# Two weight loads in the place of a matrix not yet written, and a conversion one frame earlier, in a kernel of attention, soft experts and a feed-forward layer

## The chip, the cores and the metric

The kernel runs on one core of a Trainium2 chip. The metric is the time of one execution on the device, in microseconds. TensorE (PE) does the matrix products, VectorE (DVE), ScalarE (ACT) and GpSimd (POOL) the elementwise work, and SyncE (SP) issues nearly all transfers between the chip's memory (HBM) and the core's on-chip memory (SBUF). PE's results land in a small separate memory (PSUM).

## The reference

Attention over 4 batches and 8 heads (576 tokens, 64 channels) that keeps the 32 largest scores of each row, then a layer of 8 soft experts with 4 slots each, then a feed-forward layer on every token. `w_in` and `w_out` of the last one arrive as 64-bit floats.

```python
scores = scale * np.matmul(q, k.transpose(0, 1, 3, 2))
kth = np.partition(scores, -top_k, axis=-1)[..., -top_k:-top_k + 1]
attn = softmax(np.where(scores >= kth, scores, -1e9))      # then x = attn @ v
...
logits = x @ phi                                    # 2304 x 32
d = softmax(logits, axis=0); c = softmax(logits, axis=1)
h = np.maximum((d.T @ x)[e] @ w1[e], 0.0)           # each of 8 experts, 4 slots
slot_out[e] = h @ w2[e]
x = c @ slot_out
...
h = x @ w_in                                        # 512 x 2048
g = np.where(h >= 1, h, np.where(h <= -1, 0, (h + 1) ** 2 / 4))
return g @ w_out                                    # 2048 x 512
```

## The kernel before

**Attention.** The 32 heads are handled as 16 pairs. A table, `ORDER`, is one frame of a software pipeline written out by hand: each entry is an operation (a letter and numbers) and a last letter a, b or c, which says how many frames behind the newest pair that operation works. Frames 0 to 18 run it over the 16 pairs. On PE, ACT, DVE and POOL the order of the table is the order of the program there; the order of the rest, and that of the whole tail, is set by the tile framework's scheduler.

**The conversion of `w_in`.** Its 16 blocks of 128 x 512 are converted from 64-bit to 32-bit floats beside attention, one block a frame, by the entries c0 to c6: c0 and c1 on ACT (L213, L215), c2 on ACT (L217, which also issues the load of the next block into the buffer `x64`, L192), c3 on POOL (L219), c4 on DVE (L221), c5 and c6 on POOL (L223, L225). c6 also writes the converted block to HBM (`cv_d`, L205), whence it is loaded again later. `x64` and the result buffer `tr` are one each (the `cv_slots`).

**The weight loads.** `wload` loads the weights in a fixed list, `worder`, each load 512 KB, numbered w_0, w_1, ... 32 of `w1` (w_0 to w_31), 32 of `w2` (to w_63), then two of converted `w_in` (w_64, w_65), two blocks of `w_out` (w_66, w_67), six more of `w_in` (w_68 to w_73) and 14 more of `w_out`. All are issued by SP in this order, into places taken from the list `wfree`. During attention 13 places of their own exist (`slots_a`), and each frame issues two loads until they are full, in the seventh frame. The last pair frees further places: six buffers of the attention inputs at its operation S00, three more and a score buffer at X40, and a score buffer each at some T. After the loop come `cv_slots` (2) and `half_slots` (4); then attention closes (`att.close`, which waits for its last readers, PE's `moe_ps` of L618 among them) and three more places come free (`wB`). From there on `ring`, the list of places in the order they were filled, is used again from its start (L742).

**The tail.** PE computes the experts' first layer (`h1`, L804), their second (`so_0` and `so_1`, L823). Beside `so_1` runs `mix`: it transposes the logits (`lt_ps`, L764), makes their softmax on DVE and ACT, transposes the result (`c_ps`, L790), and ACT copies it into `cT`, the token-mix matrix, one tile of 128 x 2304 (9,216 bytes in each partition) that is allocated at the program's start. `m_first` (L841) multiplies the slots with a quarter of `w_in`, `m_rest` (L850) with the other three, and `m_spread` (L865) brings these into shape. The feed-forward layer is then 96 steps of a block of 384 tokens and a block f of 128 hidden units: `emit_g` makes `h_ps` on PE (L898, two PSUM buffers shared with the other small products), `rg` on ACT (L900, L901) and DVE (L902), and its high and low halves `ghl` on DVE (L904, L905); `emit_o` does nine products `o_ps` (L916). The first 32 steps alternate between two blocks of tokens. For each f, `wo_prep` converts a block of `w_out` (the same seven operations as above, on `tr_l` and `sg_l`) and splits it into `whl` (ACT L891, DVE L892), four blocks ahead (`CLA`).

## Time and profile before

| what | us |
|---|---|
| time before, median of three runs | 875.06 |
| lowest and highest of them | 874.54, 876.78 |
| span of the profiled execution | 872.0 |
| busy in it: PE, DVE, ACT, POOL | 821.5, 685.8, 644.8, 485.4 |

The span is the time from the first to the last instruction of one profiled execution; the median of the runs stands 3.06 us over it. In the timeline the frames of attention fill the span up to about 565 us, the experts' layers and the mix lie between 565 and 616, the first 32 steps of the feed-forward layer, in which `w_out` is converted, between 616 and 715, and the other 64 behind. A reader starts with the engines' shares, then asks in which stretch which engine waits, and for whom.

### The profile page before, as it was taken

To read this page: it belongs to the slowest core of one execution; us is meant where nothing else is said; L and a number is where in the kernel's file an instruction comes from. 1 tells how busy PE (TensorE), PEld (TensorE's weight loads), DVE (VectorE), ACT (ScalarE), POOL (GpSimd) and SP (SyncE) were. 2 spreads that over 40 slices of the span, in tenths; PEclk is the share of its full clock that TensorE was granted. 3 is DMA by queue.
4 is the path that set the end of the run, shared out by engine and by line. 5 is a ranking of instruction groups with operands and counts; after the bars stand their busy time and mean duration, and the time that the engine had idled before them with its cause. 6 is when DMAs were issued, how large, how long until landed. Compare 5 with 4: busy or idle time off the path is not lost.

```text
span 872.0 us, 17711 instructions
## 1 busy us (share of the span) xinstructions
PE 821.5 (94%) x5695; PEld 674.7 (77%) x5695; DVE 685.8 (79%) x3084; ACT 644.8 (74%) x1292; POOL 485.4 (56%) x494
## 2 busy tenths in 40 slices
PE   4889999999999999999999999799698899999996
PEld 3678989988989988988988988632266678888885
DVE  6999999988999989999989994103389995666663
ACT  5688999988998988998988987412578766545453
POOL 2577888877888877888877774100467740000000
PEclk9799999999999999999999999899799999999999
DMA  8453563553353353353452536699940001001001
GB/s 240 124 152 96 165 176 98 156 157 89 103 142 92 112 133 89 102 142 87 117 134 78 157 101 205 206 343 386 399 175 1 0 2 73 37 0 38 1 37 40
DMA packets 49461, 108.59 MB, mean 125 GB/s; under 512 B 8304, under 2 KB 8304, under 8 KB 49360
## 3 DMA queue, kind: packets, MB, share of 16 engines
q1 hardware_dynamic: 49040, 106.73, 40.2%
q8 instruction: 47, 0.77, 0.4%
q10 hardware_dynamic: 320, 0.66, 0.3%
q14 instruction: 54, 0.44, 0.2%
HBM read 70.70 MB, written 8.91 MB: 91 GB/s over the span
## 4 chain that ended last, share of the span: by engine, by line
PE 78%; DVE 10%; DMA 6%; ACT 3%; POOL 1%; issue 1%; ACTq 0%; POOLq 0%; SPq 0%; DVEq 0%
PE s_ps L311 20%; PE o_ps L916 17%; PE av_ps L485 14%; PE pt_ps L457 7%; PE s_ps L413 4%; PE av_ps L486 3%; PE rem_ps L230 3%; DMA w<-in_moe_w_dram 2%; DMA w<-in_moe_w_out_dram 2%; PE h L804 2%; DVE cand L338 2%; PE moe_ps L569 2%; DMA w<-cv_d 1%; PE h_ps L898 1%; PE xT_ps L534 1%
## 5 line engine op out<-in xcount | busy, mean ns | idle before, releaser
L311 PE MATMUL s_ps<-kh,q 128*128 128x288 f32 x640 | 208.1, 342 | 16.4 <-DVE q L266 9.0
L916 PE MATMUL o_ps<-whl,ghl 128*128 128x512 f32 x864 | 216.9, 395 | 5.0 <-DVE ghl L904 4.0
L916 PEld LDWEIGHTS o_ps<-whl,ghl 128*128 128x128 f32 x864 | 159.1, 188 | 44.7 <-DVE ghl L904 7.1
L445 POOL TENSOR_TENSOR ssb<-ssb,pen 128x576 f32<-128x576 f32 x141 | 180.4, 1284 | 18.3 <-ACT pen L442 15.8
L311 PE MATMUL s_ps<-kl,q 128*128 128x288 f32 x640 | 181.2, 299 | 0.0
L338 DVE MAX8 cand<-ssb 128x8 f32<-128x82 f32 (+1 forms) x1008 | 164.2, 228 | 5.0 <-ACT ssb L329 4.0
L311 PEld LDWEIGHTS s_ps<-kh,q 128*128 128x128 f32 x640 | 123.6, 193 | 34.7 <-DVE q L266 9.4
L485 PE MATMUL av_ps<-v_sb,ptb 128*128 128x65 f32 (+1 forms) x1280 | 147.1, 261 | 0.4 <-ACT xT L547 0.4
L485 PEld LDWEIGHTS av_ps<-v_sb,ptb 128*128 128x128 f32 (+1 forms) x1280 | 141.1, 181 | 5.2 <-issue 2.6
L311 PEld LDWEIGHTS s_ps<-kl,q 128*128 128x128 f32 x640 | 124.4, 194 | 0.3
L422 DVE MAX8 l<-s_ps 128x8 f32<-128x576 f32 x144 | 109.2, 758 | 18.3 <-PE s_ps L413 17.9
L442 ACT ACTIVATE pen<-ssb,kb 128x576 bf16<-128x576 f32 x141 | 110.3, 792 | 4.5 <-POOL kb L438 3.3
L329 ACT COPY ssb<-s_ps 128x576 f32<-128x576 f32 x144 | 91.1, 641 | 25.3 <-PE s_ps L311 21.8
L448 ACT ACTIVATE ssb<-ssb,nm 128x576 f32<-128x576 f32 x141 | 109.0, 785 | 0.6 <-POOL ssb L445 0.6
L900 ACT ACTIVATE rg<-h_ps,half 128x384 f32<-128x384 f32 x96 | 55.2, 579 | 71.0 <-PE h_ps L898 70.8
L396 POOL TENSOR_SCALAR mb<-ssb,top 128x576 bf16<-128x576 f32 x48 | 83.3, 1736 | 19.2 <-DVE top L345 9.2
L902 DVE SCALAR_TENSOR_TENSOR rg<-h_ps,rg 128x384 f32<-128x384 f32 x96 | 52.9, 554 | 47.4 <-ACT rg L901 47.1
L467 ACT COPY ptb<-pt_ps 128x512 f32<-128x512 f32 x144 | 82.4, 598 | 3.3 <-PE av_ps L485 3.3
L457 PE MATMUL pt_ps<-ident,ssb 128*128 128x128 f32 x576 | 84.3, 273 | 0.2
L398 DVE TENSOR_SCALAR_CACHE_REDUCE mb<-ssb,top 128x576 bf16<-128x576 f32 x96 | 75.8, 802 | 0.0
L345 DVE MAX8 top<-cand 128x8 f32<-128x56 f32 x432 | 73.5, 207 | 0.1
L457 PEld LDWEIGHTS pt_ps<-ident,ssb 128*128 128x128 f32 x576 | 68.7, 142 | 1.3 <-ACT ptb L467 0.8
(160 smaller groups left out, 1311.7 us busy)
## 6 DMA issues: line engine op xcount, KB each, us to landing
w<-in_moe_w_dram SPq DMA_DIRECT2D x60, 512.0 KB, 6.7
q<-qst SPq DMA_DIRECT2D x60, 160.0 KB, 3.1
kh<-kst SPq DMA_DIRECT2D x60, 144.0 KB, 2.5
kl<-kst SPq DMA_DIRECT2D x60, 144.0 KB, 2.9
x<-in_moe_w_in_dram SPq DMA_DIRECT2D x16, 512.0 KB, 3.9
w<-in_moe_w_out_dram SPq DMA_DIRECT2D x16, 512.0 KB, 9.3
v_sb<-in_v_dram SPq DMA_DIRECT2D x16, 325.0 KB, 2.9
raw_t<-in_q_dram SPq DMA_DIRECT2D x15, 320.0 KB, 3.7
```

The source lines that it names most:

```text
L311: nc.tensor.matmul(s[:, hf, :HS], a, w, start=(n == 0), stop=(n == len(terms) - 1), skip_group_check=True)
L329: nc.scalar.copy(st[u]["ssb"][:, j], st.pop((u, j))[:, :, :HS])
L338: nc.vector.max(st[u]["cand"][:, j, 8 * g:8 * g + 8], row(u, j)[:, S * g // NSEG:S * (g + 1) // NSEG])
L396: nc.gpsimd.tensor_scalar(st[u]["mb"][:, j], row(u, j), t_u, None, op0=ALU.is_ge)
L422: nc.vector.max(st[u]["l8"][:, j], st.pop((u, j))[:, :, :HS])
L442: nc.scalar.activation(pen, row(u, j), AF.Relu, bias=st[u]["kb"][:, j:j + 1], scale=-BIG)
L445: nc.gpsimd.tensor_tensor(row(u, j), row(u, j), st.pop((u, "pen", j)), op=ALU.subtract)
L448: nc.scalar.activation(row(u, j), row(u, j), AF.Exp, bias=st[u]["nm"][:, j:j + 1], scale=0.125)
L457: nc.tensor.transpose(pt[:, c, :], pr[:, c * P:(c + 1) * P], ident)
L467: nc.scalar.copy(ptb, st.pop((u, "pt", j)))
L485: nc.tensor.matmul(o, pj[:, c, sl], v_sb[:, 4 * jj + c, :], start=(c == 0), stop=False)
L916: nc.tensor.matmul(pos[t][n], a[:, sl], w, start=(f == 0 and k == 0), stop=(f == NF - 1 and k == 2))
```

## The change

Three things are changed.

The first conversion block begins one frame earlier: the entries c0, c1 and c3 go from b to a, and c2, c4, c5 and c6 from c to b. All 16 blocks move with it, so the last is finished one frame earlier, too.

When the last c6 has been written, the two `cv_slots` are given to `wfree` and loads are issued into them at once, in place of after the loop.

`cT` is split into two halves of 4,608 bytes in each partition, `cT0` and `cT1`, in a pool of their own, and they are allocated in `mix`, where they are first written. Up to there their places are two entries at the head of `wfree` (`loan`), so w_0 and w_1 are loaded into them. These two places are not put into `ring`.

```diff
--- before.py
+++ after.py
@@ -56,14 +56,14 @@
 NV = 2
 CLA = 4
 ORDER = '''
-Y30b z4b E00b Q30c A11c X21b P11b T40c S00a md M31b H1c A20c Y21b Q31c K20b c4c U01b E01b C00a
-G00a K21b K30b c2c L4b S01a Q40c U11b N3b C01a R4c X31b Y31b A21c E10b S10a T00b T01b G01a B2b
-c5c P21b M40b H2c P20b E11b C10a K31b L0a O40b U21b S11a C11a Q00b A30c N0a B3b M00a X40b G10a
-Q01b U20b R0b P30b G11a Y40b L1a M10a A31c T10b S20a H3c T11b c6c E20b E21b R1b N4b S21a M01a
+Y30b z4b E00b Q30c A11c X21b P11b T40c S00a md M31b H1c A20c Y21b Q31c K20b c4b U01b E01b C00a
+G00a K21b K30b c2b L4b S01a Q40c U11b N3b C01a R4c X31b Y31b A21c E10b S10a T00b T01b G01a B2b
+c5b P21b M40b H2c P20b E11b C10a K31b L0a O40b U21b S11a C11a Q00b A30c N0a B3b M00a X40b G10a
+Q01b U20b R0b P30b G11a Y40b L1a M10a A31c T10b S20a H3c T11b c6b E20b E21b R1b N4b S21a M01a
 C20a M11a A40c C21a Q10b A41c U30b N1a K40b H4c B4b X00a S30a Q11b P31b lDc Y00a T20b md G20a
 T21b z0a md lNc R2b C30a X10a lYc K00a P40b Y10a lEc lXc E30b X01a S31a O01a A00b A01b G21a
 U31b z1a lCc Y01a X11a E31b mc C31a Q20b L2a K01a Q21b G30a M20a z2a K10a md U40b Y11a md
-z3a H0b G31a S40a c0b T30b M21a c1b K11a L3a E40b T31b mc B0a P00a O21a mc c3b R3b C40a
+z3a H0b G31a S40a c0a T30b M21a c1a K11a L3a E40b T31b mc B0a P00a O21a mc c3a R3b C40a
 B1a X20a M30a P10a mc U00a U10a mc P01a N2a Y20a G40a A10b X30a
 '''.split()
 GA = 2
@@ -80,7 +80,7 @@
     make_identity(nc, ident)
     nbig = cpool.tile([P, P], BF16, name="nbig")
     nc.scalar.mul(nbig, ident, -BIG)
-    cT = cpool.tile([P, NT], F32R, name="cT")
+    p_ct = ctx.enter_context(tc.tile_pool(name="p_ct", bufs=1))
     lall = cpool.tile([P, S], F32, name="lall")
     acc = cpool.tile([P, P], F32, name="acc")
     run_s = cpool.tile([P, 1], F32, name="run_s")
@@ -128,7 +128,8 @@
     half_slots = [((p_hold, "xu", 1), (p_qkv, "v_sb", NV))] + [((p_hold, "mb", NMB),) * 2]
     half_slots += [((p_hold, "ptb", 4),) * 2] * 2
     ssb_slot = whole(p_ssb, "ssb", NSSB)
-    wfree = list(slots_a)
+    loan = [whole(p_ct, f"cT{n}", 1) for n in range(2)]
+    wfree = loan + slots_a
     ring = []
 
     def slot_tiles(slot, name, dtype):
@@ -145,7 +146,8 @@
             if slot is None:
                 return
             wfree.remove(slot)
-            ring.append(slot)
+            if slot not in loan:
+                ring.append(slot)
             full, parts = slot_tiles(slot, f"w_{wnext[0]}", I32 if l == 4 else F32)
             if l == 0:
                 src = w1[e, c * P:(c + 1) * P, :].rearrange("p (n f) -> p n f", n=2)
@@ -659,6 +661,9 @@
                 i = pi + min(pi, NWE) + (k == "d")
                 if i < NCV:
                     conv_op(i, int(name[1]))
+                    if (i, name[1]) == (NCV - 1, "6"):
+                        wfree.extend(cv_slots)
+                        wload(99)
         else:
             if name == "G00" and pi > 0:
                 return
@@ -711,7 +716,7 @@
             for name, k in order:
                 if 0 <= frame - k < NPAIR:
                     emit(name, frame - k)
-    wfree.extend(cv_slots + half_slots)
+    wfree.extend(half_slots)
     wload(99)
     run(moe_acc(B - 1, [(0, 2 * P), (2 * P, NR * P), (NR * P, S)], ps_s))
     siT = cpool.tile([P, NHP, NSLOT], F32, name="siT")
@@ -754,7 +759,10 @@
         axes = "abcd"[:len(shape) - 1]
         return t.rearrange(f"p ({' '.join(axes)}) -> p {' '.join(axes)}", **dict(zip(axes, shape[1:])))
 
+    cT = []
+
     def mix():
+        cT.extend(p_ct.tile([P, NT // 2], F32R, name=f"cT{n}", tag=f"cT{n}", bufs=1) for n in range(2))
         wide = [P, NR + 1, B, NSLOT]
         lt = mix_tile("lt", F32, wide)
         for rows in (range(NR), (NR,)):
@@ -789,7 +797,7 @@
                     n = P if r < NR else REM
                     nc.tensor.transpose(ps[:, r % NR, :n], c4[:n, r].rearrange("p a b s -> p (a b s)"), ident[:n, :n])
                 w = len(rows) * n
-                nc.scalar.copy(cT[:, b * S + rows[0] * P:b * S + rows[0] * P + w],
+                nc.scalar.copy(cT[b // 2][:, b % 2 * S + rows[0] * P:b % 2 * S + rows[0] * P + w],
                                ps.rearrange("p a b -> p (a b)")[:, :w])
 
     nc.vector.tensor_scalar_add(run_s, run_s, 1e-9)
@@ -895,7 +903,7 @@
     def emit_g(s_):
         t, f = s_
         ph = ps_m.tile([P, 512], F32, name="h_ps", tag="m_ps")[:, :BLK]
-        nc.tensor.matmul(ph, m4[f // 4][:, f % 4 * P:(f % 4 + 1) * P], cT[:, t * BLK:(t + 1) * BLK], start=True, stop=True)
+        nc.tensor.matmul(ph, m4[f // 4][:, f % 4 * P:(f % 4 + 1) * P], cT[t // 3][:, t % 3 * BLK:(t % 3 + 1) * BLK], start=True, stop=True)
         r, g = (x[:, :BLK] for x in ring_tile("g", g_slots, "rg", F32))
         nc.scalar.activation(r, ph, AF.Relu, bias=half, scale=0.5)
         nc.scalar.activation(r, r, AF.Square)
```

The line numbers of the changed kernel are greater by 2 from about L130 on, by 5 in the 700s, and by 8 from `mix` on.

The change moves instructions, as the programs' orders show. The first place is SP's queue at the end of attention, before and then after: `cv_d15` is the write of the last converted block, w_n a weight load.

```order
L167 DMA w_27_9209<-in_moe_w1_dram 128x1024
L167 DMA w_28_9288<-in_moe_w1_dram 128x1024
L205 DMA cv_d15_112<-tr_9166 128x512
L167 DMA w_29_9290<-in_moe_w1_dram 128x1024
L167 DMA w_30_9292<-in_moe_w1_dram 128x512
L167 DMA w_30_9293<-in_moe_w1_dram 128x512
L167 DMA w_31_9296<-in_moe_w1_dram 128x512
L167 DMA w_31_9297<-in_moe_w1_dram 128x512
L167 DMA w_32_9300<-in_moe_w2_dram 128x512
L167 DMA w_32_9301<-in_moe_w2_dram 128x512
L167 DMA w_33_9304<-in_moe_w2_dram 128x512
```

```order
L207 DMA cv_d15_114<-tr_8847 128x512
L169 DMA w_27_9092<-in_moe_w1_dram 128x1024
L169 DMA w_26_9088<-in_moe_w1_dram 128x1024
L169 DMA w_32_9298<-in_moe_w2_dram 128x512
L169 DMA w_32_9299<-in_moe_w2_dram 128x512
L169 DMA w_28_9094<-in_moe_w1_dram 128x1024
L169 DMA w_29_9140<-in_moe_w1_dram 128x1024
L169 DMA w_33_9302<-in_moe_w2_dram 128x512
L169 DMA w_33_9303<-in_moe_w2_dram 128x512
L169 DMA w_30_9199<-in_moe_w1_dram 128x1024
L169 DMA w_31_9224<-in_moe_w1_dram 128x1024
L169 DMA w_34_9306<-in_moe_w2_dram 128x512
```

The write of `cv_d15` now stands ahead of w_26 and w_27 where it stood behind w_28. w_32 and w_33 are issued in the midst of the w1 loads, into the conversion's two buffers.

The second place is PE in `so_1`, at the two parts of `lt_ps` (`so_sb` is the result of `so_0`), before and then after.

```order
L823 MATMUL so_1_9745<-w_49_9439,h1T_1_9619 32x512
L823 MATMUL so_1_9745<-w_50_9441,h1T_1_9619 32x512
L831 MATMUL soT_ps_9667<-ident_62,so_sb_9665 128x128 x4
L764 MATMUL lt_ps_9677<-ident_62,lall_70 128x128 x4
L823 MATMUL so_1_9745<-w_51_9443,h1T_1_9619 32x512
L823 MATMUL so_1_9745<-w_48_9437,h1T_1_9619 32x512
L823 MATMUL so_1_9745<-w_49_9439,h1T_1_9619 32x512
L823 MATMUL so_1_9745<-w_50_9441,h1T_1_9619 32x512
L823 MATMUL so_1_9745<-w_51_9443,h1T_1_9619 32x512
L232 MATMUL lt_ps_9683<-ident_62,lall_70 64x128
L230 MATMUL lt_ps_9683<-ident_62,lall_70 64x128
L823 MATMUL so_1_9745<-w_52_9445,h1T_1_9619 32x512
```

```order
L831 MATMUL so_1_9749<-w_51_9445,h1T_1_9621 32x512
L831 MATMUL so_1_9749<-w_48_9439,h1T_1_9621 32x512
L831 MATMUL so_1_9749<-w_49_9441,h1T_1_9621 32x512
L831 MATMUL so_1_9749<-w_50_9443,h1T_1_9621 32x512
L831 MATMUL so_1_9749<-w_51_9445,h1T_1_9621 32x512
L831 MATMUL so_1_9749<-w_52_9447,h1T_1_9621 32x512
L839 MATMUL soT_ps_9669<-ident_62,so_sb_9667 128x128 x4
L772 MATMUL lt_ps_9681<-ident_62,lall_72 128x128 x4
L831 MATMUL so_1_9749<-w_53_9449,h1T_1_9621 32x512
```

The transposes of `so_sb` and `lall` now stand behind a second round of products with w_48 to w_51 and the first with w_52. The transposes into `c_ps`, which stood among the products with w_56 to w_60, now stand behind the first with w_60 and later.

The third place is the start of the steps. On ACT, `rg` is the activation of a step, `tr_l` and `sg_l` belong to the conversion of w_out, before and then after:

```order
L843 CAST m4_0_9396<-m_ps0_9789 128x512
L891 CAST whl_9805<-tr_l_9796 128x512
L217 ACTIVATE sg_l_9809<-w_67_9477 128x512
L900 ACTIVATE rg_9846<-h_ps_9844,half_75 128x384
L900 ACTIVATE rg_9855<-h_ps_9853,half_75 128x384
L901 ACTIVATE rg_9846<-rg_9846 128x384
L901 ACTIVATE rg_9855<-rg_9855 128x384
L891 CAST whl_9817<-tr_l_9808 128x512
L900 ACTIVATE rg_9876<-h_ps_9874,half_75 128x384
```

```order
L851 CAST m4_0_9402<-m_ps0_9793 128x512
L908 ACTIVATE rg_9850<-h_ps_9848,half_77 128x384
L908 ACTIVATE rg_9859<-h_ps_9857,half_77 128x384
L909 ACTIVATE rg_9850<-rg_9850 128x384
L909 ACTIVATE rg_9859<-rg_9859 128x384
L899 CAST whl_9809<-tr_l_9800 128x512
L219 ACTIVATE sg_l_9813<-w_67_9479 128x512
L908 ACTIVATE rg_9880<-h_ps_9878,half_77 128x384
L909 ACTIVATE rg_9880<-rg_9880 128x384
L899 CAST whl_9821<-tr_l_9812 128x512
```

The four instructions on `rg` now stand ahead of the first `whl` cast. On PE, between the step (1,1) of the feed-forward layer, whose last products are the first row here, and the next steps, after:

```order
L924 MATMUL o_ps1_2_9930<-whl_9821,ghl_9925 128x512
L906 MATMUL h_ps_9974<-cT0_9678,m4_0_9402 128x384
L906 MATMUL h_ps_10004<-cT0_9678,m4_0_9402 128x384
L906 MATMUL h_ps_10022<-cT0_9678,m4_0_9402 128x384
L906 MATMUL h_ps_10053<-cT0_9678,m4_1_9403 128x384
L924 MATMUL o_ps1_0_9928<-whl_9833,ghl_9980 128x512 x2
```

Before, there was one `h_ps` at a time between the steps there:

```order
L916 MATMUL o_ps1_2_9926<-whl_9817,ghl_9921 128x512 x2
L898 MATMUL h_ps_9970<-cT_69,m4_0_9396 128x384
L916 MATMUL o_ps1_0_9924<-whl_9817,ghl_9921 128x512
L916 MATMUL o_ps1_1_9925<-whl_9817,ghl_9921 128x512
L916 MATMUL o_ps1_2_9926<-whl_9817,ghl_9921 128x512
L898 MATMUL h_ps_10001<-cT_69,m4_0_9396 128x384
L916 MATMUL o_ps0_0_9883<-whl_9829,ghl_9954 128x512 x2
L916 MATMUL o_ps0_1_9884<-whl_9829,ghl_9954 128x512 x2
```

Four `h_ps` now follow each other. The products of `m_rest` (`m_ps1`), which were 24 in a row, now have products `o_ps` of the first two steps between the last of them.

## Rows read from the trace of the kernel before

**Rows 1.** Two lines of the page: the busy share of the 16 DMA engines in 40 equal slices of the span (21.8 us each, in tenths), and the chain of work that ended last, by engine.
```profile
DMA  8453563553353353353452536699940001001001
...
PE 78%; DVE 10%; DMA 6%; ACT 3%; POOL 1%; issue 1%; ACTq 0%; POOLq 0%; SPq 0%; DVEq 0%
```

**Rows 2.** The table by stretches. A row has the stretch in us, its length, then busy us and number of instructions of PE, PE's weight loads, DVE, ACT and POOL, the clock granted to PE as a share of the full one, the busy share of the DMA engines, and GB/s.
```profile
28.00:60.00 32.00, 26.09 (x167) 20.62 (x166) 31.83 (x174) 26.75 (x49) 22.87 (x27) 0.93 0.35 95
...
544.00:552.00 8.00, 7.33 (x59) 6.43 (x59) 0.67 (x3) 4.86 (x13) 3.70 (x3) 1.00 0.44 131
...
575.00:590.00 15.00, 15.00 (x113) 4.68 (x106) 2.07 (x3) 2.75 (x4) 0.00 (x0) 1.00 1.05 389
...
615.00:620.00 5.00, 3.89 (x12) 1.86 (x12) 1.04 (x5) 3.45 (x6) 2.88 (x2) 1.00 1.04 388
620.00:625.00 5.00, 1.09 (x4) 0.30 (x2) 2.34 (x3) 1.40 (x3) 3.72 (x4) 0.81 1.05 394
625.00:630.00 5.00, 2.64 (x10) 0.86 (x13) 2.89 (x6) 4.55 (x10) 1.83 (x2) 0.50 1.03 411
630.00:635.00 5.00, 5.00 (x22) 1.44 (x16) 0.44 (x2) 1.03 (x3) 2.08 (x2) 0.66 1.03 409
...
651.00:711.00 60.00, 53.52 (x219) 39.46 (x220) 55.58 (x88) 46.75 (x88) 45.31 (x32) 1.00 0.00 1
```

**Rows 3.** What SP's DMA queue waited for between 556 and 570 us: us in total, times, longest.
```profile
SPq L167 <- PE moe_ps L618: 6.6, 1, 6.6
```

**Rows 4.** The timeline of SP's DMA queue from 556 to 640 us: start, us from the first issue of the row to the end of the last, line, what is loaded, how many.
```profile
556.49 45.10 SPq L167 DMA_DIRECT2D w<-in_moe_w_dram  x39
...
607.99 1.69 SPq L167 DMA_DIRECT2D w<-in_moe_w_out_dram  x2
```

**Rows 5.** The timeline of PE from 594 to 636 us: start, us, line, output and inputs, shape, how many; in brackets the idle time before the row and what ended it.
```profile
601.09 2.37 PE L823 MATMUL so<-w,h1T 128*32 128x512 f32 x12 [0.29 <-DMA w<-in_moe_w_dram]
603.90 1.05 PE L823 MATMUL so<-w,h1T 128*32 128x512 f32 x2 [0.44 <-DMA w<-in_moe_w_dram]
605.88 0.83 PE L790 MATMUL c_ps<-ident,c 128*128 128x128 f32 x5 [0.93 <-DVE c L784]
...
616.77 3.70 PE L841 MATMUL m_ps<-w,so 128*128 128x512 f32 x8 [0.71 <-DVE so L835]
622.41 0.62 PE L898 MATMUL h_ps<-cT,m 128*128 128x384 f32 x2 [1.94 <-DVE m L844]
627.36 0.69 PE L898 MATMUL h_ps<-cT,m 128*128 128x384 f32 x1 [4.33 <-DVE rg L902]
627.98 6.29 PE L850 MATMUL m_ps<-w,so 128*32 128x512 f32 x24
```

**Rows 6.** The timeline of ACT from 594 to 640 us, columns as before.
```profile
616.08 0.66 ACT L213 ACTIVATE tr_l<-w 128x512 f32<-128x512 f32 x1 [0.73 <-DMA w<-in_moe_w_out_dram]
...
624.19 0.62 ACT L891 CAST whl<-tr_l 128x512 fp32r<-128x512 f32 x1 [3.10 <-POOL tr_l L225]
...
625.28 1.03 ACT L900 ACTIVATE rg<-h_ps,half 128x384 f32<-128x384 f32 x2
626.20 0.92 ACT L901 ACTIVATE rg<-rg 128x384 f32<-128x384 f32 x2
```

**Rows 7.** Groups of PE's instructions between 651 and 711 us: line, operation, shape, how many | busy us, mean ns of one | idle us before them and what ended it.
```profile
L916 PE MATMUL o_ps<-whl,ghl 128*128 128x512 f32 x193 | 50.3, 401 | 4.2 <-DVE ghl L904 3.5 <-DVE ghl L905 0.2
L898 PE MATMUL h_ps<-cT,m 128*128 128x384 f32 x22 | 7.3, 346 | 2.4 <-DVE rg L902 2.4
```

**Rows 8.** The timeline of POOL from 700 to 713 us: the last product of the conversion of a w_out block.
```profile
710.52 1.17 POOL L225 TENSOR_TENSOR tr_l<-tr_l,sg_l 128x512 f32<-128x512 f32 x1
```

**Rows 9.** The timeline of ACT from 541 to 553 us: the first operation of the last conversion of w_in.
```profile
544.65 0.69 ACT L213 ACTIVATE tr<-x 128x512 f32<-128x512 f32 x1
```

**Rows 10.** The timeline of DVE from 548.2 to 549.5 us: DVE's operation of the same conversion.
```profile
548.49 0.43 DVE L221 TENSOR_SCALAR tr<-tr 128x512 int32<-128x512 int32 x1
```

**Rows 11.** The timeline of DVE from 30 to 42 us: the row with the longest idle time before it.
```profile
36.98 0.25 DVE L338 MAX8 cand<-ssb 128x8 f32<-128x82 f32 x1 [0.17 <-ACT ssb L329]
```

**Rows 12.** The timeline of POOL from 24 to 42 us: its first row.
```profile
26.54 1.73 POOL L396 TENSOR_SCALAR mb<-ssb,top 128x576 bf16<-128x576 f32 x1 [5.32 <-DVE top L345]
```

**Rows 13.** Groups of DVE's instructions between 720 and 860 us, where no w_out block is converted any more; columns as in the groups of PE.
```profile
L905 DVE TENSOR_TENSOR ghl<-rg,ghl 128x384 fp32r<-128x384 f32 x62 | 34.6, 558 | 2.1
L902 DVE SCALAR_TENSOR_TENSOR rg<-h_ps,rg 128x384 f32<-128x384 f32 x62 | 34.5, 557 | 42.6 <-ACT rg L901 42.6
L904 DVE CAST ghl<-rg 128x384 fp32r<-128x384 f32 x62 | 22.3, 360 | 4.4
```

**Rows 14.** The same for 634 to 711 us, beside the conversions on POOL.
```profile
L905 DVE TENSOR_TENSOR ghl<-rg,ghl 128x384 fp32r<-128x384 f32 x26 | 22.5, 868 | 0.6
L904 DVE CAST ghl<-rg 128x384 fp32r<-128x384 f32 x28 | 17.6, 634 | 1.1
```

**Rows 15.** The timeline of PE from 636 to 716 us: where the seventh step begins.
```profile
651.01 2.39 PE L916 MATMUL o_ps<-whl,ghl 128*128 128x512 f32 x9 [0.18 <-DVE ghl L905]
```

**Rows 16.** Groups of POOL's instructions between 610 and 712 us: the conversions of the 16 blocks of w_out.
```profile
L219 POOL TENSOR_SCALAR tr_l<-tr_l 128x512 f32<-128x512 f32 x16 | 26.0, 1627 | 76.3 <-ACT tr_l L213 76.3
L223 POOL TENSOR_TENSOR tr_l<-tr_l 128x512 int32<-128x512 int32 x16 | 22.0, 1374 | 10.9 <-DVE tr_l L221 8.6 <-ACT whl L891 1.3 <-ACT rg L901 1.1
L225 POOL TENSOR_TENSOR tr_l<-tr_l,sg_l 128x512 f32<-128x512 f32 x16 | 20.0, 1252 | 4.7 <-ACT sg_l L217 4.1
```

## The prediction

> **What bounds the kernel now.** I read the page first. In the chain of work that ended last, TensorE (PE) holds 78% of the span, VectorE (DVE) 10% and the DMA queues 6% [rows 1]. So the attention frames, which are most of the span, are PE's, and a change of weight loads can't touch them unless it disturbs another engine there. The row of DMA tenths says where transfers matter: 3 to 6 through the frames, 9 in the four slices from about 568 us on [rows 1]. The table by stretches sharpens that. From 575 to 590 the 16 DMA engines are full (share 1.05) at 389 GB/s, and from 615 to 635 it is still 388 to 411 [rows 2]. A load of 512 KB is 524,288 bytes, so at 389 GB/s it takes 1.35 us, and two of them 2.7 us.
>
> The stretch before it has holes. SP's waits show one of 6.6 us on the last `moe_ps` of attention (L618, the closing of the attention pools) [rows 3]; the loads queued before it had landed by then, and everything from w_34 on stands behind it. SP makes its last 39 issues of MoE weights from 556.49 on and those of the first two blocks of w_out only at 607.99 [rows 4]. What waits for them is seen on the engines: PE waits 0.29 and 0.44 us for MoE weights at 601.09 and 603.90 [rows 5], and ACT begins the first conversion of a w_out block at 616.08, after 0.73 us on that block's DMA [rows 6].
>
> The last thing to read is what that late start costs. PE makes the first h_ps at 622.41, waits 4.33 us for DVE's `rg` before the third (627.36), and then runs m_rest for 6.29 us [rows 5], at a granted clock of 0.81, 0.50 and 0.66 in the three stretches from 620 to 635 [rows 2], so much of it at 1.2 instead of 2.4 GHz. From 651 to 711 PE idles another 4.2 + 2.4 = 6.6 us, nearly all of it on DVE's `ghl` and `rg` [rows 7], while DVE is busy 55.58 of 60 us [rows 2]. After that the w_out conversions are over (the last one's product on POOL starts at 710.52 [rows 8]). The end is thus set by when PE has done its steps up to about 711, and the idle 6.6 us is all that a better supply can take away there.
>
> **The change, part by part.** *The loan.* Two more weight loads now go into the place of the mix matrix early in attention, 15 before the last pair in place of 13, so every place that comes free later takes a weight two numbers further on. When SP meets the long wait, w_34 and w_35 have been issued and the first load behind it is w_36. Slots are reused at the same distance as before, and the transfers behind the wait are bound by bandwidth, so each weight from there on lands as the one two places before it did: 2.7 us earlier. The Trainium skill, DMA: Bandwidth & Descriptors, section Bandwidth (Where 436 GB/s comes from), says that a transfer from HBM is bound by about 358 GB/s per core; two loads would then be an estimated 2.9 us, but the trace has 388 to 411 GB/s here [rows 2], so the measurement decides.
>
> The two extra loads are paid for in the seventh and eighth frame, where the DMA engines are some four tenths busy [rows 1] and nothing of attention is due at once. Price 0; at worst an attention load is late by the one in front of it, 1.35 us; a gain there has no reason, since nothing is taken away.
>
> *The conversion one frame earlier, its end.* The seven operations of the last conversion leave the last frame, where ACT has L213 at 544.65 (0.69 us) [rows 9] and DVE L221 at 548.49 (0.43 us) [rows 10]. PE is busy 7.33 of 8 us there [rows 2], so little is to be had: 0 to 0.3 us of gain, I take 0. The write of cv_d15 and the x64 load of conversions move with it, and SP's queue is in order, but it has no load behind them that is due in that frame. The two conversion buffers then hold weights some 20 us before they are needed; this makes the two loads' place and no time of its own.
>
> *The conversion one frame earlier, its start.* In exchange the first frames get the work. From 28 to 60 us DVE is the bound (31.83 of 32 us busy [rows 2]), and its share is one more L221, 0.43 us [rows 10], less the little idle time it has, as the 0.17 us at 36.98 [rows 11]. ACT's and POOL's operations lie in idle time (POOL waits 5.32 us for DVE before 26.54 [rows 12]). Cost 0.43 - 0.17 = 0.26, up to 0.4; if ACT's two copies land in front of DVE's input they add 0.69 and about as much again, so 1.5 at worst. I take 0.3, since that row has POOL waiting for DVE and not the reverse.
>
> *The tail's order.* The order of PE is rearranged where the weights now come sooner. PE does six products of `so_1` more before `lt_ps`, so the mix chain starts about 1.2 us later (12 such products take 2.37 us [rows 5]), but `so_1` no longer waits: 0.29 + 0.44 us on DMA and 0.93 us on the `c` of the mix before 605.88 [rows 5] are filled or gone. m_first (616.77) comes 0.29 + 0.44 + 0.93 = 1.66 us earlier, at 615.1. ACT reaches the first w_out block when both that (2.7 earlier) and its own queue allow: the mix copies and the copy of `so_1` now stand before it, so between 1.66 and 2.7, I take 2.2. The first h_ps, which needs m_first, the cast and DVE's subtraction, moves by the same, 2.2 us, to 620.2.
>
> *The third h_ps.* Before, ACT's two `rg` stood behind a `whl` cast that began at 624.19, after 3.10 us on POOL [rows 6]; that is PE's wait of 4.33. Now `rg` stands ahead of `whl`. The third h_ps needs a buffer back, so it comes after one h_ps (0.31), both L900 (1.03), one L901 (0.46) [rows 5, 6] and one L902 of 0.56 us [rows 13], 2.4 us after the first: about 622.5, 4.9 us earlier. PE's lead at m_rest is then 4.9 us. Which clock m_rest meets I leave as it was: PE idles less before it (2.4 - 0.6 us between the h_ps in place of 4.33), but it idles. At the full clock its 6.29 us would be little more than half; up to 3 us that I keep for a rival.
>
> *Where the lead is lost again.* The new order of PE has, after the step (1,1), four h_ps in a row, with two PSUM buffers to hold them. The third and fourth must wait until ACT and DVE have emptied one: L900, L901 and L902 are 0.52 + 0.46 + 0.56 = 1.5 us, and for the fourth the same again with the L904 and L905 of a step ahead of it on DVE, 0.634 + 0.868 us [rows 14], 3.0 us. That sum, 4.5 us, takes PE's lead of 4.9 nearly whole, so after six steps PE stands near 651, where the seventh begins now [rows 15]. DVE, ACT and POOL do keep theirs: the conversion chain starts 2.2 us earlier and no longer loses about 2 to the `rg` behind `whl`, which makes about 4 us.
>
> *Behind 651.* PE's idle 6.6 us there are waits on DVE [rows 7]. With DVE 4 us further ahead, 4 of them go; the rest stay, as does all work after 711.
>
> Sum, against the profiled execution's own span of 872.0 us: 0 (loan) + 0 (drain) + 0.3 (fill) - 4 (supply behind 651) + 0.2 for what the four h_ps may cost DVE, which waits for them = -3.5, a span of 868.5. The median of the runs before, 875.06, stands 3.06 us over that span, so **871.5 us**. Between ends: the supply 3 to 5, the fill 0 to 0.4, so 869.8 to 872.4.
>
> **Rivals.** *Only the lead of the start.* POOL and DVE together set the pace from 634 to 711, and the end moves by what their first operation moved, 2.2 us, less the 0.3 of the fill: 873.1 (872.4 to 874.9). For it: DVE's `ghl` operations L904 and L905 take 634 and 868 ns on average beside POOL, and 360 and 558 ns behind 720 us, where POOL is quiet [rows 13, 14], and DVE is 93% busy. Against it: DVE also has `rg` waits that the new ACT order removes. The Trainium skill, SBUF — State Buffer, section Who interferes with whom, says that DVE and GpSimd lock a shared port pair for a whole instruction. Fully in turn, POOL's 1.627 + 1.374 + 1.252 us [rows 16] and DVE's 2 x (0.360 + 0.558) + 0.43 would be 6.5 us for a block of w_out; the trace has 32 POOL instructions, 10.7 blocks, in 60 us [rows 2], 5.6 us each. So the trace bears the rule out in part only, and by it the end would be this rival's.
>
> *More.* PE keeps its lead: the four h_ps find their buffers empty, because DVE's queue is short at that point, and m_rest meets the full clock. Then the row of waits behind 651 empties, and the idle 6.6 us are gone whole: 875.06 - 6.6 + 0.3 = 868.8 (867.4 to 869.8).
>
> *Slower.* The four h_ps cost more than the lead: PE waits for two rounds of ACT and DVE, the clock falls again in that hole, and the o_ps steps behind run at the lower level. Six steps are then done 1.7 us later than before, at 652.7; DVE, which waits for h_ps, loses its lead with it, and with the 0.3 of the fill the time is 877.1 (876 to 878.5). It decides if the waits in that place sum to more than 4.9 + 1.7 us.
>
> *The loads are no earlier.* The long wait of SP moves with the loads, or the ring makes the second half wait for a slot, so that w_66 lands when it did: 875.0, with the fill 875.3.
>
> **How the numbers follow.** A measurement of this kernel can tell about 0.3% from no change, 2.6 us: faster is under 872.4, slower over 877.7. Chances: forecast 0.45, more 0.15, only the start 0.25, no earlier loads 0.08, slower 0.07. Faster is the first two, 0.60; the third and fourth and the smaller part of the last are the middle, 0.35; slower 0.05. The range reaches over the forecast, most of more and most of only the start: 868.0 to 874.6.
>
> **What would show it.** Right: SP's one wait on `moe_ps` has w_36 behind it; the first w_out conversion on ACT starts near 613.9; the third h_ps near 622.5; POOL's last product about 4 us before 710.52; PE's idle time from 651 on down to some 3 us. Wrong in the fill: the frames' end (the wait on `moe_ps`) later by over 0.5 us. Wrong in the tail: m_ps0 no earlier than 616, or PE's six steps done after 652. The forecast falls if POOL's last product is less than 3 us earlier.

## The result, and the profile after

The change makes the kernel slower: 887.65 us, median of four runs (887.07 to 890.34), beside 875.92 for the kernel before on the same chip (874.54 to 879.27), a ratio of 1.0129, 95% interval 1.0103 to 1.0155. The forecast was 871.5, the range 868.0 to 874.6. The profiled execution has a span of 885.2 us, 13.2 more than before.

First, where in the program the 13.2 us arise. The starts are read from PE's timelines of both kernels, the products behind 651 and 711 from the groups of PE's instructions.

| place | before | after | later by |
|---|---|---|---|
| end of attention (si_ps) | 567.94 | 568.32 | 0.38 |
| so_0 done (first soT_ps) | 595.75 | 599.51 | 3.76 |
| first c_ps | 605.88 | 610.87 | 4.99 |
| m_first | 616.77 | 619.32 | 2.55 |
| third h_ps | 627.36 | 626.98 | -0.38 |
| o_ps begun by 651 | 51 | 27 | 24 products |
| o_ps from 711 on | 621 | 668 | 47 products |
| last product of the conversion on POOL | 710.52 | 712.77 | 2.25 |

At the third h_ps these two executions are even, and everything is lost behind it. Of before, these are the groups of o_ps from 616 to 651 us and from 711 us on (count, busy us, mean ns, idle us before them):

```profile
L916 PE MATMUL o_ps<-whl,ghl 128*128 128x512 f32 x51 | 13.6, 405 | 0.8 <-DVE ghl L904 0.4 <-DVE ghl L905 0.4
...
L916 PE MATMUL o_ps<-whl,ghl 128*128 128x512 f32 x621 | 153.4, 392 | 0.3 <-DVE ghl L904 0.3
```

After, the same two stretches, and between them the groups from 651 to 711, which answer to [rows 7] (the 7.6 us of h_ps count in a wait of 3.17 us that ends ahead of 651):

```profile
L924 PE MATMUL o_ps<-whl,ghl 128*128 128x512 f32 x27 | 8.5, 461 | 0.0
...
L924 PE MATMUL o_ps<-whl,ghl 128*128 128x512 f32 x171 | 47.4, 429 | 5.2 <-DVE ghl L912 5.2
L906 PE MATMUL h_ps<-cT,m 128*128 128x384 f32 x17 | 6.6, 408 | 7.6 <-DVE rg L910 7.6
...
L924 PE MATMUL o_ps<-whl,ghl 128*128 128x512 f32 x668 | 166.3, 393 | 0.1
```

From 740 to 800 us both kernels run 268 products of PE in 60 us, 0.224 us each. So the 24 products that are missing at 651 are worth 5.4 us, and 47 of o_ps and 7 of h_ps (72 in place of 65) from 711 on are 12.1 us of the 13.2. POOL's conversions end only 2.25 us later: the conversions kept their pace, and the steps fell behind them.

The table by stretches, after, columns as in [rows 2]:

```profile
568.00:575.00 7.00, 6.54 (x34) 1.61 (x38) 0.68 (x3) 0.27 (x1) 0.00 (x0) 0.56 0.77 248
575.00:590.00 15.00, 15.00 (x128) 4.68 (x123) 1.38 (x2) 2.75 (x4) 0.00 (x0) 1.00 1.00 367
...
640.00:651.00 11.00, 6.00 (x16) 3.91 (x16) 8.73 (x14) 9.60 (x18) 6.36 (x5) 0.77 0.22 89
651.00:656.00 5.00, 4.73 (x12) 3.46 (x12) 4.97 (x7) 2.96 (x6) 3.09 (x3) 0.50 0.00 0
...
661.00:666.00 5.00, 1.69 (x8) 1.11 (x6) 3.64 (x4) 2.78 (x6) 4.49 (x4) 1.00 0.00 0
666.00:671.00 5.00, 4.20 (x13) 3.40 (x14) 3.85 (x8) 2.68 (x5) 2.02 (x2) 0.66 0.00 0
...
651.00:711.00 60.00, 50.44 (x192) 38.67 (x192) 49.16 (x74) 42.42 (x77) 41.67 (x31) 0.90 0.00 0
```

Before, two of these stretches are the following, and 651 to 711 is in [rows 2]:

```profile
568.00:575.00 7.00, 6.86 (x62) 2.10 (x66) 0.42 (x2) 0.27 (x1) 0.00 (x0) 0.96 0.91 311
...
640.00:651.00 11.00, 10.15 (x40) 6.83 (x39) 9.86 (x16) 9.01 (x17) 7.65 (x6) 1.00 0.14 55
```

From 640 to 651 and from 651 to 711 PE idles 5.00 + 9.56 us, before 0.85 + 6.48, so 7.2 us more. It does 208 products in place of 259, 51 fewer, worth 11.4 us. Some 4 us of that are not idling; they go with the lower granted clock, at which 12 products take 4.73 us of the stretch from 651 to 656.

PE's timeline after, from 599 us on, answers to [rows 5]; the long waits behind 640 are new:

```profile
603.70 0.30 PE L234 MATMUL lt_ps<-ident,lall 128*64 128x128 f32 x1
...
605.91 1.04 PE L831 MATMUL so<-w,h1T 128*32 128x512 f32 x2 [0.31 <-DMA w<-in_moe_w_dram]
607.26 2.41 PE L831 MATMUL so<-w,h1T 128*32 128x512 f32 x12 [0.30 <-DMA w<-in_moe_w_dram]
610.87 0.83 PE L798 MATMUL c_ps<-ident,c 128*128 128x128 f32 x5 [1.20 <-DVE c L792]
...
619.32 3.67 PE L849 MATMUL m_ps<-w,so 128*128 128x512 f32 x8 [0.76 <-ACT tr_l L215]
624.39 0.62 PE L906 MATMUL h_ps<-cT,m 128*128 128x384 f32 x2 [1.40 <-DVE m L852]
626.98 0.69 PE L906 MATMUL h_ps<-cT,m 128*128 128x384 f32 x1 [1.97 <-DVE rg L910]
...
641.53 0.44 PE L906 MATMUL h_ps<-cT,m 128*128 128x384 f32 x1 [1.99 <-DVE rg L910]
...
650.32 1.15 PE L906 MATMUL h_ps<-cT,m 128*128 128x384 f32 x2 [3.17 <-DVE rg L910]
...
666.80 2.92 PE L924 MATMUL o_ps<-whl,ghl 128*128 128x512 f32 x6 [4.11 <-DVE ghl L912]
...
685.78 0.44 PE L906 MATMUL h_ps<-cT,m 128*128 128x384 f32 x1 [3.37 <-DVE rg L910]
```

Before, no wait of PE behind 640 is longer than this one:

```profile
694.72 0.44 PE L898 MATMUL h_ps<-cT,m 128*128 128x384 f32 x1 [1.74 <-DVE rg L902]
```

What stands ahead of the 4.11 us is seen on DVE, after:

```profile
656.57 0.55 DVE L910 SCALAR_TENSOR_TENSOR rg<-h_ps,rg 128x384 f32<-128x384 f32 x1
...
662.32 1.37 DVE L223 TENSOR_SCALAR tr_l<-tr_l 128x512 int32<-128x512 int32 x1 [2.93 <-POOL tr_l L221]
663.62 0.35 DVE L912 CAST ghl<-rg 128x384 fp32r<-128x384 f32 x1
...
665.45 1.30 DVE L912 CAST ghl<-rg 128x384 fp32r<-128x384 f32 x1
```

DVE sits 2.93 us at an operation of the conversion (L223), which waits for POOL, and the `ghl` operations that PE waits for, the one at 665.45 last, stand behind it in DVE's order. The last `rg` ahead of them (L910) was done at 657.12, so their input had long been there. ACT waits alike, 2.40 us before 656.41 at a conversion (L215) that needs DVE's `whl` operation done, ahead of its next `rg`.

Last, the loads. SP's waits from 500 to 580 us and its timeline, after, answer to [rows 3] and [rows 4]:

```profile
SPq L169 <- PE moe_ps L620: 8.4, 1, 8.4
...
SPq L169 <- PE h L812: 4.7, 4, 2.5
```

```profile
603.22 4.33 SPq L169 DMA_DIRECT2D w<-cv_d  x4
608.64 1.69 SPq L169 DMA_DIRECT2D w<-in_moe_w_out_dram  x2
```

In this execution the first two blocks of w_out are issued 0.65 us later than before, not 2.7 earlier, and ACT's first operation on them starts at 617.85 in place of 616.08 [rows 6]. How much of that is the change's is told further down, with e6.

### The profile page after: what moved, and what is told of

Read it like the earlier page. It is cut to its first block, busy times and chain, and to the rows that moved or that the text cites. A ratio compares the mean times of both kernels' runs of the same rounds, so it can differ in the third digit from the quotient of the medians.

```text
span 885.2 us, 17750 instructions
## 1 busy us (share of the span) xinstructions
PE 830.6 (94%) x5695; PEld 681.8 (77%) x5695; DVE 689.0 (78%) x3084; ACT 646.5 (73%) x1292; POOL 483.5 (55%) x494
## 4 chain that ended last, share of the span: by engine, by line
PE 82%; DVE 9%; DMA 4%; ACT 2%; issue 1%; POOL 1%; ACTq 0%; DVEq 0%; POOLq 0%; SPq 0%
PE o_ps L924 20%; PE s_ps L313 20%; PE av_ps L487 14%; PE pt_ps L459 7%; PE s_ps L415 4%; PE av_ps L488 3%; PE rem_ps L232 3%; PE h L812 2%; DVE cand L340 2%; DMA w<-cv_d 2%; PE moe_ps L571 2%; PE h_ps L906 2%; DMA w<-in_moe_w_dram 1%; PE xT_ps L536 1%; PE rem_ps L234 1%
## 5 line engine op out<-in xcount | busy, mean ns | idle before, releaser
L924 PE MATMUL o_ps<-whl,ghl 128*128 128x512 f32 x864 | 221.7, 402 | 5.3 <-DVE ghl L912 5.2
L924 PEld LDWEIGHTS o_ps<-whl,ghl 128*128 128x128 f32 x864 | 164.5, 193 | 46.1 <-DVE ghl L912 7.7
L910 DVE SCALAR_TENSOR_TENSOR rg<-h_ps,rg 128x384 f32<-128x384 f32 x96 | 53.1, 555 | 51.5 <-ACT rg L909 49.4
L221 POOL TENSOR_SCALAR tr_l<-tr_l 128x512 f32<-128x512 f32 x16 | 24.8, 1553 | 89.1 <-PE soT_ps L839 78.6
```

What stands on the lines that cost most here:

```text
L924: nc.tensor.matmul(pos[t][n], a[:, sl], w, start=(f == 0 and k == 0), stop=(f == NF - 1 and k == 2))
```

## The experiments

Ratios are against the kernel before on the same chip, with their 95% intervals. One count from the programs' orders recurs: how many blocks ACT has cast into `whl` when the 4th, 8th, ... 24th `rg` stands next in its queue. Steps alternate between two blocks of tokens, so step n uses n/2 blocks.

```
                       rg:   4   8  12  16  20  24   ratio
before                       2   4   6   9  10  12
the change                   2   4   8  10  12  15   1.0129
e2                           2   4   8  10  12  14   1.0117
e3                           2   8   9  12  14  16   1.0202
e4                           4   6   9  12  14  16   1.0128
e6                           2   5   7   9  10  13   1.0076
e7                           2   4   8  10  12  15   1.0093
e9                           2   6   8  11  13  15   1.0193
e10                          2   4   6   8  10  12   1.0031
e11                          2   4   6   9  11  13   1.0058
e12                          2   4   6   9  11  13   1.0085
e14                          2   4   6   8  10  12   1.0015
(e1, e5, e8, e13 as before)
```

**The two halves of the change.** e1 is the kernel before with the new table `ORDER` alone, e2 with the loan alone.

```diff
-    wfree = list(slots_a)
+    loan = [whole(p_ct, f"cT{n}", 1) for n in range(2)]
+    wfree = loan + slots_a
...
+            if slot not in loan:
+                ring.append(slot)
```

> The kernel before with only the conversion one frame earlier (no loan, the two conversion buffers lent after the loop as before). PE, ACT and DVE keep the tail's order of before. Order theory (the loss comes from the new order of the steps in the tail): +0.3 to +0.6 us, the extra conversion operations in the first frames, so about 876.3. Transfer theory (the loss comes from weights that are no earlier, and what waits for them): the same. A theory that the frames pay for the conversion: +3 us or more.

> The kernel before with only the loan of the matrix's place to two weight loads. The scheduler's order in the tail is then nearly that of the changed kernel (four h_ps in a row, rg ahead of whl). Order theory: most of the loss is here, +9 to +12 us, 885 to 888. Transfer theory: the loads behind the long wait are delayed as in the changed kernel, too, +9 to +12 us; this run does not tell the two apart. If the conversion's move is the cause: +1 us or less.

e1: 876.42, 0.9984 (0.9967 to 1.0001). e2: 889.43, 1.0117 (1.0094 to 1.0140). The conversion's move costs nothing that can be measured; the loan by itself carries a loss of the same size.

**PE's order, exchanged.** From m_first on, PE's order of one kernel is pinned in the other (a chain of order-only dependences over a table of positions); the other engines stay with the scheduler.

```diff
+    for engine, text in TAIL.items():
...
+        for x, y in zip(order, order[1:]):
+            tc.add_manual_dep(mine[y], mine[x].name,
+                              mybir.DependencyInfo(mybir.DependencyClass.NoSync, mybir.DependencyReason.DATA))
```

> The changed kernel, with PE's instructions from m_first on held in the order that the kernel before has (ordering edges on PE alone; ACT, DVE and POOL are ordered by the scheduler around it). Loads as in the changed kernel. Order theory: most of the loss goes, 876 to 880 us, and the idle lumps of over 3 us on PE between 640 and 690 are gone. Transfer theory: 885 to 889 us, as the changed kernel.

> The kernel before, with PE's instructions from m_first on held in the order of the changed kernel (ordering edges on PE alone), loads as before. Order theory: slower by 6 to 12 us, 882 to 888, with PE idle in lumps of over 2 us between 640 and 690. Transfer theory: 875 to 877 us.

e3: 896.02, 1.0202 (1.0185 to 1.0219). e4: 889.86, 1.0128 (1.0112 to 1.0145). PE's new order brought the whole loss into the kernel before (e4), but PE's old order made the changed kernel slower still (e3), so putting PE's order right is no cure. Neither run tells PE's order from the others', since the scheduler arranged ACT, DVE and POOL anew around it: in e4, too, ACT casts nine blocks ahead of the 12th `rg`. In e3 ACT casts eight blocks ahead of the 8th `rg`, and PE's timeline shows the price, a step that waits 16.20 us:

```profile
636.27 0.34 PE L956 MATMUL h_ps<-cT,m 128*128 128x384 f32 x1
652.80 4.05 PE L974 MATMUL o_ps<-whl,ghl 128*128 128x512 f32 x9 [16.20 <-ACT whl L949]
```

**The order of all engines, and the places.** The loan also moves every entry of `ring` by two, and with it the places that the tail's buffers `rg`/`ghl` (`g_slots`) and `whl` (`w_slots`) get. e5 is the changed kernel with the tail's places and the order of all four engines as before; e6 only with the places; e7 is the kernel before, its loads untouched, with the places that the changed kernel gives to these buffers and to the outputs `o_sb`. The edit of e7:

```diff
-    g_slots, o_slots, w_slots = ring[:8], mix_slots + ring[8:9], ring[9:9 + NF]
+    g_slots, o_slots = slots_b[1:] + [ssb_slot] + qkv_slots[:2], slots_a[12:] + slots_b[:1] + qkv_slots[2:]
+    w_slots = [ssb_slot] * 2 + cv_slots + [ssb_slot] * 3 + half_slots + [whole(wB, f"wB{n}", 1) for n in range(NB)]
+    w_slots += slots_a[:2]
```

> The changed kernel with the tail's buffers put into the places that they have in the kernel before, and with PE, ACT, DVE and POOL held in the order of before through the whole tail (ordering edges on all four). Loads and conversion as in the changed kernel. Order theory: the loss goes whole, 874 to 877.5 us. Transfer theory: 885 to 889 us.

> The changed kernel with the tail's buffers (rg, ghl, whl, o, the mix) put into the places that they have in the kernel before; the order is the scheduler's own, which then is neither that of before nor that of the changed kernel. Place theory (the loss comes from which places the loan leaves for the steps' buffers, whatever the order): 874 to 878 us. Order theory: anything between 874 and 890, by the order that comes out; PE's idle lumps and the granted clock between 636 and 700 must then go with the time. Transfer theory: 885 to 889.

> The kernel before, nothing lent and no conversion moved; only the tail's buffers rg, ghl and whl are put into the places that they have in the changed kernel. The scheduler then makes an order of PE that is near the changed kernel's. Order and place theory: slower by 8 to 14 us, 884 to 890. Transfer theory: 875 to 877.

e5: 880.06, 1.0040 (1.0024 to 1.0056). e6: 884.61, 1.0076 (1.0046 to 1.0105). e7: 885.06, 1.0093 (1.0066 to 1.0119). e7 is the strongest of the three: no load differs, ACT's counts are those of the change, and most of the loss is there. e6 is a miss for the places alone (874 to 878 expected): with the places of before the changed kernel keeps 0.76% of its 1.29%, so the places are not all of it; the order that the scheduler makes there is a third one, with seven casts ahead of the 12th `rg`. The stretches of e7 show the marks of the changed kernel:

```profile
640.00:651.00 11.00, 6.06 (x18) 3.61 (x16) 9.56 (x14) 9.74 (x20) 9.04 (x7) 0.84 0.33 134
651.00:711.00 60.00, 52.93 (x199) 39.42 (x200) 52.98 (x79) 43.38 (x81) 44.31 (x32) 0.91 0.00 1
```

In e5, with the loads of the change, most of the loss is gone, and the stretch from 651 to 711 is as before [rows 2]:

```profile
651.00:711.00 60.00, 53.58 (x220) 39.53 (x221) 54.64 (x86) 47.52 (x89) 44.83 (x31) 1.00 0.00 0
```

Its profile loses time ahead of that: the first `c_ps` waits 4.92 us there, 0.93 before. e3 and e5 have the same order of PE behind m_first; they differ in places and in the order of ACT, DVE and POOL, and stand at 1.0202 and 1.0040.

**Is an earlier supply worth anything?** e8 is the kernel before without the loads w_34 and w_35, e13 without w_52 to w_57; products that used them use another weight's tile, and the order of before is pinned.

```diff
-            for dst, sr in dmas:
+            for dst, sr in dmas if wnext[0] not in (34, 35) else []:
```

> The kernel before without the two loads w_34 and w_35 (the products with them use w_32 and w_33, so two blocks of w2 are left out of the result), with all four engines held in the order of before in the tail. It shows what weights that land two places earlier are worth when nothing else changes. The forecast's step on supply: m_first 1.7 us, the first w_out conversion 2 us earlier, the time down by 2 to 4 us. Rival (the end is set by DVE and POOL in the steps, or hidden): within 1 us of before.

> The kernel before without the six loads w_52 to w_57 (the products with them use w_44 to w_49, so six blocks of w2 are left out of the result), all four engines held in the order of before in the tail. Unlike w_34 and w_35 these stand in the stretch where the transfers are bound by bandwidth, so w_64 and all behind it must land about 8 us earlier, and neither PE nor ACT waits for a weight between 600 and 617. It tells what an earlier supply is worth with the order held. The forecast's step (an earlier start of the steps is handed on to the end): m_first 1.5 to 2.5 us earlier and the time down by as much, 0.2 to 0.3%. Rival (the steps from 634 on set the end by DVE and POOL, whatever their start): within 0.1% of before.

e8: 877.30, 0.9998 (0.9979 to 1.0018). Though SP has two loads fewer to issue, it reaches the loads of `cv_d` at 602.35 (before 602.43). It waited longer at h1, which reads the places that the ring wants back; SP's waits from 556 to 615 us, before and in e8:

```profile
SPq L167 <- PE h L804: 2.7, 6, 0.8
```

```profile
SPq L234 <- PE h L874: 5.9, 8, 2.1
```

But the 90 products of h1 took 11.82 us in that execution and 10.49 in that of before, so this profile doesn't say how much of the wait comes from the loads.

e13: 879.76, 1.0027 (1.0007 to 1.0047). Here the supply is early: SP issues the first w_out blocks at 604.71 (before 607.99), and `so_1` has no wait on a DMA left. PE's timeline shows what takes its place:

```profile
601.41 0.66 PE L901 MATMUL soT_ps<-ident,so_sb 128*128 128x128 f32 x4
...
611.50 1.38 PE L860 MATMUL c_ps<-ident,c 128*128 128x128 f32 x5 [3.87 <-DVE c L854]
```

From soT_ps to the first c_ps are 10.09 us, and before 10.13 (595.75 to 605.88). That stretch is the mix chain on DVE and ACT, and here its length is the same though the weights come earlier. PE merely waits 3.87 us for it in place of 0.93 [rows 5]. The granted clock from 600 to 615 is then 0.84, before 1.00, this row of `c_ps` takes 1.38 us in place of 0.83, and from soT_ps to m_first are 23.40 us in place of 21.02: in this profile the earlier supply did not bring m_first forward.

**Bunched steps, or conversions ahead?** e9 is the changed kernel with h_ps and o_ps on PE in the order of the code, so that no four h_ps stand in a row. e10 has `CLA` at 1, so that the code takes up a block of w_out one block ahead of the steps and not four. e11 has both, e12 is the kernel before with both, and e14 the kernel before with `CLA` at 1.

```diff
-CLA = 4
+CLA = 1
...
-        nc.tensor.matmul(ph, m4[f // 4][:, f % 4 * P:(f % 4 + 1) * P], cT[t // 3][:, t % 3 * BLK:(t % 3 + 1) * BLK], start=True, stop=True)
+        tc.keep_in_program_order(nc.tensor.matmul(ph, m4[f // 4][:, f % 4 * P:(f % 4 + 1) * P], cT[t // 3][:, t % 3 * BLK:(t % 3 + 1) * BLK], start=True, stop=True))
```

> The changed kernel, with the step products on PE (h_ps and o_ps) held in the order in which the code writes them: one h_ps between two steps, never four in a row. ACT's order still has 8 whl casts (blocks of w_out converted) ahead of the 12th rg, as the changed kernel (the kernel before: 6). Bunching theory (four h_ps in a row, then many o_ps, make the idle lumps): most of the loss goes, 876 to 880. Conversions-ahead theory (what delays rg on DVE, ACT and POOL is w_out blocks converted ahead of the steps that need them): most of the loss stays, 883 to 890.

> The changed kernel with the conversions of w_out written one block ahead of the steps in place of four (CLA = 1). ACT's order then has 6 whl casts ahead of the 12th rg, as the kernel before; PE's order is the scheduler's, with pairs of h_ps at most. Conversions-ahead theory: 877 to 881, near the run with the order of before (880). Bunching theory: also down, since the four in a row are gone, but pairs stay: 878 to 885. If only the transfers count: 886 to 889.

> The changed kernel with both: PE's steps in the written order and the conversions one block ahead. 6 whl casts ahead of the 12th rg, one h_ps at a time. Both theories: 874 to 880; if it is under the kernel before, the loan pays once the order is held.

> The kernel before with PE's steps in the written order and the conversions one block ahead; loads as before. 6 whl casts ahead of the 12th rg. 872 to 877: at or a little under the kernel before, if an even order is what the steps need. It also is the control for the run with the same two edits in the changed kernel: the difference of the two is what the loan and the moved conversion cost or bring with the order held, -2 to +4 us.

> The kernel before with the conversions of w_out written one block ahead of the steps in place of four, the scheduler's own order. It is the control for the changed kernel with the same edit (880.3 us, 1.0031 of before): if this is within 0.2% of before, the changed kernel's remaining 0.3% is the loan's and the moved conversion's; if it is 0.3% slower itself, nothing of the remainder is theirs. I expect 876 to 880.

e9: 893.89, 1.0193 (1.0151 to 1.0234). e10: 880.28, 1.0031 (1.0008 to 1.0053). e11: 881.99, 1.0058 (1.0036 to 1.0080). e12: 884.16, 1.0085 (1.0055 to 1.0115). e14: 879.98, 1.0015 (0.9995 to 1.0035).

Without bunches the changed kernel is slower, with conversions held back most of the loss is gone. The cleanest pair is e9 and e11: both are the changed kernel with PE's steps in the same order and no bunch, they differ in `CLA` alone, and stand at 1.0193 and 1.0058. Their stretch from 651 to 711, e9 and then e11:

```profile
651.00:711.00 60.00, 48.98 (x176) 34.50 (x177) 48.16 (x68) 38.93 (x71) 43.37 (x32) 0.89 0.00 0
```

```profile
651.00:711.00 60.00, 52.90 (x204) 38.23 (x203) 53.70 (x80) 42.97 (x81) 42.58 (x31) 0.94 0.00 1
```

What the bunch costs by itself is open: no run takes it away without another order of PE's steps or other conversions. PE in e10, 651 to 711, the stretch and two groups:

```profile
651.00:711.00 60.00, 53.19 (x204) 35.98 (x204) 53.12 (x81) 44.08 (x82) 42.46 (x32) 1.00 0.00 0
```

```profile
L924 PE MATMUL o_ps<-whl,ghl 128*128 128x512 f32 x180 | 48.1, 407 | 3.6 <-DVE ghl L912 2.1 <-DVE ghl L913 1.0
L906 PE MATMUL h_ps<-cT,m 128*128 128x384 f32 x20 | 7.4, 378 | 2.2 <-DVE rg L910 2.0
```

From 640 to 726 its longest wait of PE is 1.07 us and the granted clock 1.00. With e14 as its control, the change stands at 1.0031 against 1.0015 once the conversions are held, and with e12 as that of e11 at 1.0058 against 1.0085: both pairs of intervals overlap, and whether a rest of the loan's cost remains is open. e12 is a miss for the account by conversions: it has as few casts ahead as before and still costs 0.85%. PE's order as the code has it has a price of its own, with no loan in it, and that price is in e9, too.

## Why the prediction was wrong

**The step that failed: DVE, ACT and POOL get 4 us ahead, and PE's waits behind 651 fall by as much (the -4 of the sum).** The prediction says "With DVE 4 us further ahead, 4 of them go", from 6.6 us of idle time to some 3. By the stretches it is 9.56 us, before 6.48, and with 640 to 651 it is 14.56 in place of 7.33; the granted clock fell to 0.90. The lead in time did not come: ACT's first operation on w_out starts 1.77 us later, POOL's last product ends the conversions 2.25 us later, where the forecast was to fall if it came less than 3 us earlier. What grew is the lead of the conversions over the steps: eight blocks are cast before the 12th `rg` in place of six. A conversion that is put early stands, in the order of DVE or ACT, in front of a `ghl` or `rg` that PE waits for, as at 662.32. The prediction had no price for that. That places alone lead to such an order, without any change of loads, is shown by e7; that most of the loss goes when the conversions are held, by e10, by e11 beside e9, and in another way by e5. How two places further on lead the scheduler to that order was not traced.

**The loan's gain (each weight 2.7 us earlier): near right, though the profile after hides it.** In that execution h1 ran at a granted clock of 0.56 from 568 to 575 us, before 0.96: its 90 products took 12.99 us against 10.49. SP waited for h1 4.7 us in place of 1.8 from 500 to 580 us. e6 has the loads of the change, and there h1 took as long as before. Before, and then e6, on PE:

```profile
567.94 0.48 PE L719 MATMUL si_ps<-ident,acc 128*128 128x128 f32 x1 [0.47 <-DVE acc L626]
...
568.77 10.49 PE L804 MATMUL h<-w,siT 128*32 128x512 f32 x90
```

```profile
571.93 0.47 PE L724 MATMUL si_ps<-ident,acc 128*128 128x128 f32 x1 [0.47 <-DVE acc L628]
...
572.76 10.49 PE L811 MATMUL h<-w,siT 128*32 128x512 f32 x90
...
620.31 5.37 PE L848 MATMUL m_ps<-w,so 128*128 128x512 f32 x8 [0.76 <-ACT tr_l L215]
...
629.67 0.45 PE L907 MATMUL h_ps<-cT,m 128*128 128x384 f32 x1 [1.97 <-DVE rg L911]
```

SP issues the first blocks of w_out at 609.60 in e6. From the end of attention (si_ps) that is 37.67 us, and 40.05 before [rows 4], so 2.4 us less. The rival that the loads are no earlier, at 0.08, is not what this shows. This rests on one profile of each kernel, and e6 differs from the change in the places of the tail's buffers.

**m_first 1.66 us earlier: mis-sized, and the first place where the gain was lost.** From the end of attention m_first comes after 48.38 us in e6, before after 48.83, so 0.45 earlier. In the profile after it is 2.55 later, of which h1 makes 2.50. The mix chain starts later by more than the 1.2 us of the forecast: so_0 is done 3.76 us later, which less 0.38 for attention and 2.50 for h1 leaves 0.88, and from soT_ps to the second half of lt_ps are 4.19 us (599.51 to 603.70), before 2.86 (595.75 to 598.61), 1.33 more; 2.2 in all. And the waits of `so_1` on DMA (0.28, 0.31 and 0.30 us) and on `c` (1.20) were not filled. e13 shows the reason: with the order of before, weights that come earlier still have PE wait there for the mix chain.

**The third h_ps 2.4 us after the first: right** (624.39 to 626.98 is 2.6; before 4.95). `rg` ahead of `whl` does what was said, and it pays back the 1.98 us by which the first h_ps is late. The lead at m_rest is 0.4 us in the profile after, and 1.7 in e6 (57.74 us from the end of attention, before 59.42), not 4.9.

**Four h_ps in a row cost 4.5 us: less, 3.17.** They are the two at 646.64 and the two at 650.32. The 1.99 us before 641.53 stand at an h_ps ahead of the four, where PE waited 0.26 in the kernel before; the prediction has no term for it. That both together, 5.16, are near the forecast's 4.5 is chance. Less the lead of 0.4 they put PE 4.8 us behind at 651, and the count of products says 5.4.

**The fill (0.3 us): not told apart from nothing.** Attention ends 0.38 us later in the profile after, but with the frames of before it ends anywhere from 567.29 (e8) to 572.14 (e13), and e1 measures no cost.

**The rival slower** had the place and the clock right (holes in the first steps, o_ps at the lower level) and the sign; it charged it to the bunch of four h_ps alone and priced it at 877.1. e9, without the bunch, is no faster.

Two slips of the prediction change nothing: the row of DMA tenths has 9 in three slices, not four [rows 1], and the ends of its terms (supply 3 to 5, fill 0 to 0.4, and the 0.2) give 870.3 to 872.7, not 869.8 to 872.4.

No variant is clearly faster than the kernel before: the best is e1, whose interval reaches 1.

## What to carry to other kernels

A change of buffers is also a change of order, wherever a scheduler or a ring of places sits in between: move the places alone, without the benefit, and time that first. Work that feeds a later step is no gain when it is done early in an in-order queue that also feeds the step that is due; count how far ahead it runs. And before an earlier load is worth anything, ask which other chain ends at the same point.

## What was not expected of the hardware

In the profile after, each of PE's four longest waits behind 640 goes with a stretch at a lower clock: with the 1.99 us the granted clock is 0.77 from 640 to 651, after the 3.17 us it is 0.50 from 651 to 656, after the 4.11 us it is 0.66 from 666 to 671, after the 3.37 us 0.83 from 681 to 691. Before, with waits of at most 1.74 us, it is 1.00 from 640 to 711. The length of one wait doesn't decide it: in e12, where the longest wait from 651 to 661 is 1.27 us, it is 0.83 there. So such waits can cost more than their length, here some 4 us beside 7.2 of idling.

The same 90 products of h1 took 10.49 us in the profiled execution of before and in that of e6, 11.73 in e1, 12.99 after and 13.00 in e10, though e6 is 0.76% slower than before and e10 0.31%. An execution's own h1 is no measure of a change, and a difference of 2.5 us in one profile there has to be held against the medians.
